# The second layer of eight experts as fifteen block products, with a fixed instruction order

## The chip, the core and the metric

The kernel runs on one core of a Trainium2 chip. A core has a matrix engine (TensorE, PE in the profile; its weight loads are PEld), three engines for elementwise work (VectorE = DVE, ScalarE = ACT, GpSimd = POOL), a queue engine (SyncE = SP) and 16 DMA engines that move data between the chip's main memory and the on-chip memory. Each engine takes its instructions in the order in which they stand in its own queue and waits on semaphores for the others. The metric is the device time of one execution in microseconds; three runs of the kernel before give a median of 415.86 us (415.71 to 416.34).

## The reference

An attention block with a decaying state gives a matrix `x` of 3072 tokens by 384 channels. Then each token goes to one of eight experts, 384 tokens to each, chosen by a greedy walk over all (token, expert) scores in falling order, and each expert is two matrix products with a relu between.

```python
def _moe_ref(x, w_gate, w1, w2):            # N, D, E, F = 3072, 384, 8, 1024
    cap = N // E
    logits = x @ w_gate
    order = np.argsort(-logits.flatten())
    for idx in order:                       # greedy walk
        tok, e = int(idx) // E, int(idx) % E
        if assigned[tok] >= 0 or counts[e] >= cap:
            continue
        assigned[tok] = e
        counts[e] += 1
    for e in range(E):
        mask = assigned == e
        h = np.maximum(x[mask] @ w1[e], 0.0)
        out[mask] = h @ w2[e]
```

## The kernel before

The first 165 us are the attention (class `Mild`) and, beside its end, 256 tokens of one expert chosen ahead of time (`Experts.early`); this change leaves both nearly alone. What follows is the part in question: seven experts with 384 tokens, then the remaining 128 tokens of the expert chosen early.

One full expert is, on TensorE:
- layer one, `hidden` (L1487): 8 blocks `j` of 128 hidden channels. Each is 3 matmuls with a 128x128 block of `w1` as weights and `xT`, 128 channels by 384 tokens, as the moving side, into `h_ps`; ScalarE applies the relu into `hid` (L1494).
- layer two, `result` (L1501): 3 blocks `c` of 128 tokens. Each is 8 matmuls with a 128x128 block of `hid` as weights and 128x384 of `w2` as the moving side, into `o_ps`. ScalarE copies the result to `o_sb`, and GpSimd scatters its rows to the output with an indirect DMA.
- before the last of the three, `turn` (L1477): nine transposes of the next expert's gathered tokens `xg` into `xT`.

Which expert comes next and which tokens it has is found by the class `Assignment` while the experts run. `likely_steps` (L977) is one search: three rounds of `count`, in each of which VectorE builds an indicator `ind`, TensorE counts it (`counts`, two matmul groups with VectorE's `own`, `cnt`, `wide` between them), and VectorE derives the next digit of a threshold; then two short matmuls into `st_ps` from which VectorE numbers the places. `book`, `choose` and `leave` are small VectorE steps on the result, and `leave` strikes the chosen tokens from the score table `LG`. `bound` (L1237) runs once: a matmul into `high_ps` and a reduction into `lowest`, which `book` reads. `tokens` (L1348) turns places into a list: VectorE builds `row` and `vals`, TensorE multiplies them (`some_ps`), VectorE reduces to `part`, TensorE multiplies once more (`list_ps`), and VectorE writes `tok`. `fetch` (L1473) then gathers the tokens by three indirect DMAs on GpSimd's queue, and has SP load the expert's two weight matrices of 1.5 MB each. The last search is `remainder` (L1315), which only takes what is left.

`run` (L1513) drives the experts and `later` (L1620) is the generator that yields the next one. In the attention part the order of the instructions is written out by hand (`tc.manual_schedule()`). From `x.run` on it is not: a scheduler places the search's instructions among the experts' matmuls. The weights are double buffered in two pools (`turns`), the searches' PSUM tiles share one buffer (tag `few`) and another for `counts`.

Of the kernel before, what the change touches and what calls it, by code (L numbers as in the profile page):

```python
# [688 lines left out]
class Assignment:  # L689
# [260 lines left out]
    def last_fill(self):  # L950
        out = self.remainder()
        return out["fmax"], self.tokens(out["place"])
# [290 lines left out]
    def surely(self, pool, fmax, acc, place):  # L1243
# [69 lines left out]
        self.places(pool, sel, acc, place)  # L1313

    def remainder(self):  # L1315
# [6 lines left out]
        fmax = self.outs.tile([128, 1], F32, name="fmax")  # L1322
        nc.vector.tensor_scalar(out=fmax, in0=self.last, scalar1=-1.0, scalar2=float(self.E),
                                op0=ALU.mult, op1=ALU.add)
        acc = self.outs.tile([128, self.NT], BF16, name="acc")
        place = self.outs.tile([128, self.NT], I32, name="place")
        self.places(pool, sel, acc, place)
        return dict(fmax=fmax, acc=acc, place=place)

    def places(self, pool, sel, acc, place):  # L1330

        nc, ps, NT = self.nc, self.ps, self.NT
        flat = sel.rearrange("p j i -> p (j i)")
        st_ps = ps.tile([128, 2, 2 * NT], F32, name="st_ps2", tag="few")
        nc.tensor.matmul(st_ps[:, 0, :], self.ones, flat, start=True, stop=True)
        nc.tensor.matmul(st_ps[:, 1, :], self.rest_of, flat, start=True, stop=True)
        upto = pool.tile([128, 2 * NT], F32, name="upto2")
# [10 lines left out]
    def tokens(self, place, NC=None):  # L1348

# [19 lines left out]
        self.between()  # L1369
# [36 lines left out]
def rwkv5_eagle_then_base_layer_balanced(  # L1406
# [31 lines left out]

    class Experts:
# [7 lines left out]
        def open_rest(self, ctx, **how):  # L1447
            pool = lambda name, bufs, **kw: ctx.enter_context(tc.tile_pool(name=name, bufs=bufs, **kw))
            self.h, self.o = pool("f_h", 2, **how), pool("f_o", 3, **how)
            self.ps_t, self.ps_h, self.ps_o = (pool(f"f_ps_{x}", 2, space=PSUM) for x in "tho")  # L1450

        def load_weights(self, n, fmax):
# [4 lines left out]
            w1, w2 = pool.tile([128, KD, F], F32, name="w1"), pool.tile([128, KF, DX], F32, name="w2")  # L1457
            e = nc.values_load(number[0:1, 0:1], engines=(mybir.EngineType.SP,), min_val=1, max_val=E,
                               skip_runtime_bounds_check_because="held between 1 and E")
            for t, src in ((w1, moe_w1), (w2, moe_w2)):  # L1460
                nc.sync.dma_start(t, src[ds(E - e, 1)].rearrange("o (c p) f -> p (o c) f", p=128))
            return w1, w2

# [9 lines left out]
        def fetch(self, n, fmax, tok):  # L1473
            xg = self.gather(n, tok)
            return n, xg, walk.in_order(tok), *self.load_weights(n, fmax)

        def turn(self, ahead):  # L1477
# [7 lines left out]
            return xT  # L1485

        def hidden(self, w1, xT, m):  # L1487
            hid = self.h.tile([128, KF, CAP], F32, name="hid")
            for j in range(KF):
                h_ps = self.ps_h.tile([128, CAP], F32, name="h_ps")  # L1490
                for f in range(KD):
                    nc.tensor.matmul(h_ps[:, 0:m], w1[:, f, ts(j, 128)], xT[:, f, 0:m],  # L1492
                                     start=(f == 0), stop=(f == KD - 1))
                nc.scalar.activation(hid[:, j, 0:m], h_ps[:, 0:m], AF.Relu)  # L1494
            return hid
# [5 lines left out]
        def result(self, c, hid, w2, tok, to):  # L1501
            o_ps = self.ps_o.tile([128, DX], F32, name="o_ps")
            for j in range(KF):
                nc.tensor.matmul(o_ps, hid[:, j, ts(c, 128)], w2[:, j, :], start=(j == 0), stop=(j == KF - 1))  # L1504
# [8 lines left out]
        def run(self, ahead, later, rows):  # L1513
            xT = self.turn(ahead)
            while ahead:
                _, _, tok, w1, w2 = ahead
                nb = tok.shape[1]
                ahead = next(later, None)
                hid = self.hidden(w1, xT, nb * 128)
                for c in range(nb):  # L1520
                    if c == nb - 1 and ahead:
                        xT = self.turn(ahead)
                    self.result(c, hid, w2, tok, next(rows))

        def early(self, ps, pool, w1, w2, xg, tok, rows, have):
# [18 lines left out]
            for c in range(NE):  # L1544
                o_ps = ps.tile([128, DX], F32, name="e_o_ps", tag=("y_ps", "g_ps")[c % 2])
                for j in range(KF):
                    nc.tensor.matmul(o_ps, hid[:, j, ts(c, 128)], w2[:, j, :], start=(j == 0), stop=(j == KF - 1))  # L1547
# [7 lines left out]
    with ExitStack() as whole:  # L1555
# [6 lines left out]
        with ExitStack() as part:  # L1562
# [20 lines left out]
            with tc.manual_schedule():  # L1583
# [22 lines left out]
                to = walk.in_order(tok)  # L1606
# [6 lines left out]
                for m in (2, 3, 2, 3):  # L1613
                    next(search)
                    go(m)
                go(99)
# [3 lines left out]
        def later():  # L1620
            for _ in search:
# [61 lines left out]
```

## Time and profile before

| what | us |
|---|---|
| median of three runs | 415.86 |
| the profiled run's own time | 415.83 |
| the span of the profiled execution | 414.1 |
| TensorE busy in the span | 394.4 |
| VectorE / ScalarE / GpSimd busy | 200.0 / 153.6 / 134.6 |
| one full expert, from first layer-one matmul to the next expert's | 33.4 |
| layer one's matmuls in all, 384 records | 122.2 |
| layer two's matmuls in all, 352 records | 117.6 |

The profile is one execution, taken by the hardware profiler. Lines of its group table read: source line, engine, operation, output tile and inputs, shapes, number of records, busy time, mean ns of one. A mean duration of one matmul is its latency; since matmuls are pipelined, the spacing of their starts is what a stream costs. Lines of the timeline read: start, duration, engine, line, operation, and in brackets how long the engine had been idle and what ended that. Lines of time windows list, for each engine, busy time and the number of records, then TensorE's granted clock, the share of time in which the DMA engines were busy, and GB/s. Lines of the chain of waits give the start and the length of a piece of the chain that ended last.

### The profile page before, as it was taken

The numbers are of one execution on the slowest core, as the hardware profiler recorded it, in microseconds if no ns is written. First come the engines' busy times: TensorE is split into PE (matmuls) and PEld (weight loads), VectorE is DVE, ScalarE is ACT, GpSimd is POOL, SyncE is SP. The second block draws the span as 40 slices with busy tenths as digits, with TensorE's granted clock in tenths as the row PEclk, the third lists the DMA queues.
The fourth block names the chain that finished last, engine by engine and source line by source line (L and its number), as shares of the span: only waits on it lengthen the run. The fifth ranks groups of instructions, "written<-read, shape, count | busy, mean of one in ns | idle before, by whom it ended". The sixth has DMA issues, their size and how long they took to land.

```text
span 414.1 us, 7993 instructions
## 1 busy us (share of the span) xinstructions
PE 394.4 (95%) x2981; PEld 268.3 (65%) x2981; DVE 200.0 (48%) x794; ACT 153.6 (37%) x401; POOL 134.6 (33%) x172
## 2 busy tenths in 40 slices
PE   5999999999999888999999999999999999999993
PEld 4778888888877655555556555555655655655581
DVE  5776776576885788780580381273074050010000
ACT  2597888788872312212121120221221221212120
POOL 5597878566732022004104103103002121110100
PEclk9799999999999999999999999999999999999998
DMA  9999998887591282047045137109108653350010
GB/s 123 163 154 195 197 169 153 157 169 156 123 321 41 78 298 101 2 142 258 21 180 201 38 91 291 39 10 352 38 21 311 240 173 109 138 190 5 19 39 25
DMA packets 95298, 57.25 MB, mean 138 GB/s; under 512 B 77201, under 2 KB 89490, under 8 KB 95250
## 3 DMA queue, kind: packets, MB, share of 16 engines
q1 hardware_dynamic: 91520, 47.19, 45.7%
q0 software_dynamic: 3072, 9.44, 6.4%
q8 instruction: 25, 0.41, 0.4%
q14 instruction: 23, 0.19, 0.2%
q10 hardware_dynamic: 658, 0.01, 0.1%
HBM read 47.20 MB, written 9.44 MB: 137 GB/s over the span
## 4 chain that ended last, share of the span: by engine, by line
PE 71%; DMA 12%; DVE 6%; issue 5%; ACT 2%; POOL 1%; POOLq 0%; ACTq 0%; DVEq 0%
PE h_ps L1492 21%; PE o_ps L1504 19%; DMA out_dram<-o_sb,to 11%; PE y_ps L532 7%; PE g_ps L494 5%; PE kT_ps L456 3%; PE kv_ps L511 3%; PE rT_ps L462 2%; PE x_ps L581 2%; PE e_o_ps L1547 2%; PE lg_ps L561 2%; PE xT_ps L1483 2%; ACT AT L484 1%; PE e_h_ps L1539 1%; POOL xg L1468 1%
## 5 line engine op out<-in xcount | busy, mean ns | idle before, releaser
L1492 PE MATMUL h_ps<-xT,w 128*128 128x384 f32 (+1 forms) x384 | 122.2, 469 | 0.6 <-ACT xT L1484 0.6
L1504 PE MATMUL o_ps<-w,hid 128*128 128x384 f32 x352 | 117.6, 487 | 0.0
L1504 PEld LDWEIGHTS o_ps<-w,hid 128*128 128x128 f32 x352 | 65.4, 190 | 42.4 <-issue 0.8
L1492 PEld LDWEIGHTS h_ps<-xT,w 128*128 128x128 f32 x384 | 65.6, 190 | 36.5 <-issue 3.6
L1494 ACT ACTIVATE hid<-h_ps 128x384 f32<-128x384 f32 (+1 forms) x64 | 29.7, 464 | 92.2 <-PE h_ps L1492 85.3
L484 ACT ACTIVATE AT<-ident,dd 128x128 f32<-128x128 f32 x192 | 58.7, 390 | 2.1 <-DVE dd L443 1.9
L1468 POOL DMA_INDIRECT xg<-x_rows,tok x22 | 21.3, 966 | 116.2 <-issue 58.9
L1498 POOL DMA_INDIRECT out_dram<-o_sb,to x21 | 20.8, 993 | 98.1 <-ACT o_sb L1510 66.4
L1510 ACT COPY o_sb<-o_ps 128x384 f32<-128x384 f32 x21 | 10.1, 479 | 95.5 <-PE o_ps L1504 86.8
L498 DVE COPY_PREDICATED AT<-mask,g_ps 128x512 f32<-128x512 uint8 x48 | 32.6, 734 | 12.5 <-PE g_ps L494 12.2
L889 DVE TENSOR_TENSOR own<-counts,same 128x64 f32<-128x64 f32 x21 | 4.7, 225 | 65.5 <-PE counts L901 65.5
L494 PE MATMUL g_ps<-rT,kT 48*128 48x128 f32 x384 | 28.2, 287 | 0.6 <-DVE AT L498 0.6
L431 POOL TENSOR_TENSOR kss<-krs,wk 128x384 f32<-128x384 f32 x24 | 24.3, 1015 | 10.7 <-DVE krs L340 9.0
L494 PEld LDWEIGHTS g_ps<-rT,kT 48*128 48x128 f32 x384 | 23.6, 189 | 3.8 <-PE rT_ps L462 0.8
L532 PE MATMUL y_ps<-AT,vts 128*64 128x128 f32 x384 | 25.7, 276 | 0.0
L438 POOL TENSOR_TENSOR rk<-rk,u_bc 128x384 f32<-128x384 f32 x24 | 24.2, 1008 | 3.7 <-ACT u_bc L407 1.9
L437 POOL TENSOR_TENSOR rk<-krs 128x384 f32<-128x384 f32 x24 | 24.5, 1019 | 0.0
L532 PEld LDWEIGHTS y_ps<-AT,vts 128*64 128x64 f32 x384 | 20.6, 137 | 1.0 <-issue 0.5
L550 ACT COPY x<-y_ps 128x512 f32<-128x512 f32 x24 | 14.0, 585 | 15.9 <-PE y_ps L532 15.9
L474 DVE TENSOR_TENSOR rT<-rT_ps,WR 112x512 f32<-112x512 f32 x23 | 15.8, 685 | 4.4 <-PE rT_ps L462 4.3
L462 PE MATMUL rT_ps<-ident,krs 128*112 128x128 f32 x96 | 15.3, 285 | 0.0
L581 PE MATMUL x_ps<-ident,x 112*128 112x112 f32 x96 | 13.3, 262 | 1.4 <-ACT xr L588 0.7
(270 smaller groups left out, 464.6 us busy)
## 6 DMA issues: line engine op xcount, KB each, us to landing
w<-in_moe_w_dram SPq DMA_DIRECT2D x18, 1536.0 KB, 8.3
krs<-in_k_dram SPq DMA_DIRECT2D x24, 192.0 KB, 4.1
krs<-in_r_dram SPq DMA_DIRECT2D x24, 192.0 KB, 4.7
vts<-in_v_dram SPq DMA_DIRECT2D x24, 192.0 KB, 4.5
x_rows<-xr SPq DMA_DIRECT2D x24, 192.0 KB, 2.9
xg<-x_rows,tok POOLq DMA_INDIRECT x22, 4.7
out_dram<-o_sb,to POOLq DMA_INDIRECT x21, 2.6
wp<-in_w_dram SPq DMA_DIRECT2D x2, 0.4 KB, 2.0
```

What stands on the lines that cost most here:

```text
L431: self.nc.gpsimd.tensor_mul(self.kss[:, n % self.NS].rearrange("p (g h) d -> p g h d", g=2)[:, :, :, 0:D], src, self.wk.rearrange("p (g h) ...
L437: nc.gpsimd.tensor_mul(rk, self.krs[:, n % self.NK, 1, 0:H, 0:D], self.krs[:, n % self.NK, 0, 0:H, 0:D])
L438: nc.gpsimd.tensor_mul(rk, rk, self.u_bc)
L462: nc.tensor.transpose(rT_ps[0:P, a, :], self.pair(kr[:, 1], a), self.ident)
L484: nc.scalar.mul(AT[:, z, a, :], self.ident, dd[:, h:h + 1])
L494: nc.tensor.matmul(g_ps[:, z, a, :], kT[rows, a, :], rT[rows, a, :], start=True, stop=True)
L498: nc.vector.copy_predicated(out=AT[:, z], mask=self.mask.unsqueeze(1).to_broadcast([128, HP, T]), data=g_ps[:, z])
L532: nc.tensor.matmul(yv[q * PD:(q + 1) * PD, o // 2, o % 2, :], lhsT, rhs, start=(o // 2, q) not in seen, stop=stop, skip_group_check=True)
L1468: nc.gpsimd.indirect_dma_start(out=xg[:, c, :], out_offset=None, in_=x_dram[0:within, :], in_offset=bass.IndirectOffsetOnAxis(ap=tok[:, c: ...
L1492: nc.tensor.matmul(h_ps[:, 0:m], w1[:, f, ts(j, 128)], xT[:, f, 0:m], start=(f == 0), stop=(f == KD - 1))
L1494: nc.scalar.activation(hid[:, j, 0:m], h_ps[:, 0:m], AF.Relu)
L1504: nc.tensor.matmul(o_ps, hid[:, j, ts(c, 128)], w2[:, j, :], start=(j == 0), stop=(j == KF - 1))
```

## The change

For the seven full experts the second layer is no longer 24 matmuls of 128x384. The 384x1024 matrix of hidden values is cut into 3 token blocks by 2 halves of the hidden channels (`h0` to `h5`), the 1024x384 weights into 2 halves by 3 blocks of output channels (`w0` to `w5`), and the 3x3 blocks of the result are made from fifteen products of sums of these blocks instead of eighteen products of the blocks. Each product is 4 matmuls of 128x128. The sums of hidden blocks (11 of 128x512) and of results (20 of 128x128) are made on VectorE. Ten sums of weights are made without an engine's addition: ScalarE copies one block, and a DMA on GpSimd's queue adds another block to the copy while it is moved. So that a weight block is contiguous, `w2` is laid out by blocks and loaded by six DMAs instead of one. Each group of four products shares one PSUM tile, which ScalarE copies to `res`.

```diff
+        W2_SUMS = (("W7", "w0", "w1"), ("W12", "w0", "w2"), ("W11", "w0", "w3"), ("W9", "W7", "w3"),
+                   ("W5", "W12", "w3"), ("W13", "W9", "w4"), ("W6", "W5", "w5"), ("W0", "W13", "w5"),
+                   ("W2", "W6", "w4"), ("W14", "W0", "w2"))
+        PRODUCTS = ((("p4", "h4", "w1"), ("p1", "H1", "w2"), ("p11", "H11", "W11"), ("p10", "h5", "w4")),
+                    (("p8", "H8", "w5"), ("p13", "h1", "W13"), ("p7", "H7", "W7"), ("p9", "H9", "W9")),
+                    (("p3", "H3", "w3"), ("p0", "H0", "W0"), ("p14", "h2", "W14"), ("p5", "H5", "W5")),
+                    (("p12", "H12", "W12"), ("p6", "H6", "W6"), ("p2", "H2", "W2")))
+        def w2_sums(self, w2, at):
+            for name, a, b in self.W2_SUMS:
+                t = self.sums.tile([128, KF // 2, 128], F32, name=name)
+                nc.scalar.copy(t, at[b])
+                nc.gpsimd.dma_start(out=t, in_=at[a], accum_op=ALU.add)
+                at[name] = t
+                yield
+        def hid_sums(self, at, which):
+            for name, a, op, b in which:
+                t = self.sums.tile([128, KF // 2, 128], F32, name=name)
+                nc.vector.tensor_tensor(out=t, in0=at[a], in1=at[b], op=op)
+        def products(self, left, right):
+            for group in self.PRODUCTS:
+                ps = self.ps_o.tile([128, 4, 128], F32, name="p_ps", tag="o_ps")
+                for q, (name, a, b) in enumerate(group):
+                    for j in range(KF // 2):
+                        nc.tensor.matmul(ps[:, q, :], left[a][:, j, :], right[b][:, j, :],
+                                         start=(j == 0), stop=(j == KF // 2 - 1))
+                    if q == len(group) - 1:
+                        nc.scalar.copy(res[:, n:n + q + 1, :], ps[:, 0:q + 1, :])
+                    yield res
...
-            for t, src in ((w1, moe_w1), (w2, moe_w2)):
-                nc.sync.dma_start(t, src[ds(E - e, 1)].rearrange("o (c p) f -> p (o c) f", p=128))
+            nc.sync.dma_start(w1, moe_w1[ds(E - e, 1)].rearrange("o (c p) f -> p (o c) f", p=128))
+            rows_of = moe_w2[ds(E - e, 1)].rearrange("o (j c p) (k f) -> p j k (o c) f", p=128, j=2, f=128)
+            for j in range(2):
+                for k in range(KD):
+                    nc.sync.dma_start(w2[:, j, k], rows_of[:, j, k])
```

The second part of the change puts the experts under `tc.manual_schedule()` too. `run` now counts layer one's 24 matmuls by `u` and the products by `q`, and at fixed values of both it asks `later` for the next step of the search, issues the block sums, and transposes the next expert's tokens. A step ends at a `yield`, which stands behind the TensorE instruction that the step leads to; so each search matmul has a fixed place. The first and the second full expert have plans of their own.

```diff
+        USUAL = (4, 7, 12, 19), (21, None), (1, 3, 11, 14), 8
...
+                for u in range(KF * KD):
...
+                    if f == KD - 1:
+                        nc.scalar.activation(hid[:, j, 0:m], h_ps[:, 0:m], AF.Relu)
+                        if j < KF // 2:
+                            next(sums, None)
+                            next(sums, None)
+                    if u in steps:
+                        next(later, None)
+                    if u == 5:
+                        next(out, None)
+                    if u == 8:
+                        to = walk.in_order(tok)
+                    if u == last[0]:
+                        ahead = found()
+                    if u == KF * KD - 2:
+                        for _ in sums:
+                            pass
+                        if nb == NC:
+                            self.hid_sums(left, self.FIRST_SUMS)
...
+                for q, res in enumerate(self.products(left, right)):
+                    if q in next_steps:
+                        next(later, None)
+                    if q == last[1]:
+                        ahead = found()
+                    if q == 1:
+                        self.hid_sums(left, self.SECOND_SUMS)
+                    if q == 3:
+                        self.hid_sums(left, self.THIRD_SUMS)
+                    if q == 11 or q == 14:
+                        next(out)
+                    if q == turned and ahead:
+                        xTs = self.turn(ahead)
+                    xT = next(xTs, xT)
...
+        first_plan = (2, 5, 8, 12, 14, 17, 19, 22), (None, 8), (6, 11, 13), 12
+        second_plan = (1, 3, 6, 8, 13, 20), (22, None), (1, 3, 11, 14), 9
+        with tc.manual_schedule():
+            x.run((1, xg, tok, *have["v"]), later(), (a for a in [*out_rows[2:NT - 1], None]),
+                  {"start": None, 1: first_plan, 2: second_plan})
```

`later` yields in more places, `tokens` and `remainder` are cut into steps, and the weights of the next expert are loaded as soon as its number is known, before its token list. The three scatters of an expert now come together, from one tile of 384 tokens, after the third group of result sums (`u == 5` of the next expert). The last 128 tokens keep the old second layer.

## The prediction

> **What bounds the kernel now.** I read first the page's busy table and slices, then the time windows over one expert, then the chain of waits in order of time, then the timeline of the last, small expert, which holds the one row that has the new products' shape.
>
> ```profile
> PE 394.4 (95%) x2981; PEld 268.3 (65%) x2981; DVE 200.0 (48%) x794; ACT 153.6 (37%) x401; POOL 134.6 (33%) x172
> PEclk9799999999999999999999999999999999999998
> ...
> 199.20:232.60 33.40, 33.40 (x128) 19.61 (x128) 14.21 (x74) 6.57 (x14) 5.93 (x6) 1.00 0.36 130
> ...
> 209.81 4.61 PE h_ps L1492 x14
> 214.42 0.15 PE some_ps L1365 x6
> 214.57 1.38 PE h_ps L1492 x4
> 215.96 10.42 PE o_ps L1504 x32
> 226.38 0.66 PE xT_ps L1483 x6
> ```
>
> The window 199.20 to 232.60 is one expert: TensorE (second figure) is busy for all 33.40 us at a granted clock of 1.00, VectorE 14.21, ScalarE 6.57, GpSimd 5.93, transfers 0.36 of the time. The chain there is TensorE alone, expert after expert. So the stage pays for the stream of matmul instructions, and anything that makes TensorE wait is paid in full. An f32 matmul of the source is two records here (24 of layer two make 48), a transpose one.
>
> **The products (gain).** Before: 24 matmuls of 384 columns, 48 records per expert. The chain gives 10.42 us for 32, so 0.3256 each and 15.63 us. After: 15 products of 4 matmuls of 128 columns, 120 records, each with its own weight load. That shape is in the trace: layer one of the last expert has 128 tokens.
>
> ```profile
> 396.64 5.52 PE L1492 MATMUL h_ps<-xT,w 128*128 128x128 f32 x48
> 400.85 0.28 ACT L1494 ACTIVATE hid<-h_ps 128x128 f32<-128x128 f32 x1 [0.39 <-PE h_ps L1492]
> 401.52 0.28 ACT L1494 ACTIVATE hid<-h_ps 128x128 f32<-128x128 f32 x1 [0.39 <-PE h_ps L1492]
> ```
>
> Relus follow each other by 0.67 us for 6 records: 0.1117 each, so 120 take 13.40 us. The gain is 2.23 us an expert, 15.6 us over the seven full experts. Bounds: 5.52/48 = 0.115 gives 13.8 and 12.8 us in all; a third of 0.3256 gives 13.0 and 18.2 us.
>
> The Trainium skill, "TensorE: Matmul & The Clock Gate", section "Back-to-back issue gap", speaks against the change: a stream of weight load and matmul is sustained at about 81 ns for 128 columns and 131 for 512, so small ones pay far more per column. Read linearly that is an estimated 114 ns at 384: 120 x 81 against 48 x 114 ns, 4.2 us lost an expert. The rows of this trace have the f32 shapes themselves, 0.1117 against 0.3256, almost in the ratio of the columns, and they decide.
>
> **The sums of hidden blocks and results.** 11 sums of 128x512 and 20 of 128x128 go to VectorE. No row has 128x512 from two SBUF tiles; TENSOR_TENSOR rows of 768 columns (944 ns) and 192 (344 ns) give 1.04 ns a column, 677 ns, and records overlap by some 0.07, so 0.61 each (0.55 to 0.68), and 0.21 to 0.28 for 128 columns. About 6.7 + 5 us join the 14.2: 26 of 31, so VectorE fits, but the order of its queue is now fixed, and so is the place of each search matmul on TensorE. ScalarE gets ten copies (0.585 each, the row of a 128x512 copy) and four PSUM copies for three: 6.6 becomes some 13 us. Two copies follow each of the first four relus, 0.49 + 1.17 us against a relu every 1.94: hidden; without that cover 0.3 us a relu.
>
> **Where the fixed order makes TensorE wait.** In the first full expert:
>
> ```profile
> 167.52 0.38 PE L1239 MATMUL high_ps<-ident,e_high 128*128 128x128 f32 x2
> 167.74 0.81 PE L1492 MATMUL h_ps<-xT,w 128*128 128x384 f32 x2
> 168.39 0.25 PE L901 MATMUL counts<-prop,ind 128*128 128x64 bf16 x3
> ```
>
> (a) Before, high_ps and the next search's first counts are 0.87 us apart, with layer one between: VectorE did the search's m, prop and ind first. After, both matmuls stand back to back behind layer one's sixth, and VectorE's queue puts the read of high_ps ahead of book, leave and the whole start of the search. From the spacings of those rows: high_ps to `lowest` 0.51, `lowest` twice 0.4, book 1.1, leave 1.3, cand, m, prop and low 0.9, ind to counts 0.8: 5.0 us, less 0.22 for high_ps itself, so 4.8 (3.9 to 5.2) in which layer one stands queued behind it. st_ps at the 23rd matmul adds 0.3.
> (b) The first list (some_ps) stands after the seventh product. VectorE has before it all 11 hidden sums (6.7) and the 3.1 us from `sole` to `vals`; TensorE gets there 7.1 us after st_ps: it waits 2.9. Then the token list, three gathers (spaced 1.27, landing 2.9 to 4.6 us after issue by the rows' least and usual), and the transposes placed after products 13 to 15: a further 1.3 to 2.9, the now uncovered copy of the last transposed block (0.8) included. Together 5.0 (4.2 to 5.8).
> (c) The second expert's result sums (1.75) stand between two search steps only 1.94 apart on TensorE: 1.3 (0 to 1.7).
> (d) In the five later experts the walk leaves 0.2 each, where the first two search steps meet VectorE's sums: 1.0 (0 to 4).
>
> **The sums of weights.** Ten copies, then ten accumulating 256 KB transfers on GpSimd's queue, five deep (W7, W9, W13, W0, W14), each issue waiting for the landing before it; three scatters and three gathers stand in the same queue. No row has an accumulation. Nearest:
>
> ```profile
> xg<-x_rows,tok POOLq DMA_INDIRECT x22, 4.7
> out_dram<-o_sb,to POOLq DMA_INDIRECT x21, 2.6
> ...
> 217.17 0.99 POOL L1468 DMA_INDIRECT xg<-x_rows,tok  x1 [16.21 <-issue]
> 218.46 0.96 POOL L1468 DMA_INDIRECT xg<-x_rows,tok  x1 [0.30 <-issue]
> ```
>
> An issue takes 0.97 and the next comes 1.27 later. A 192 KB scatter lands after 2.6; at the windows' 400 GB/s it moves in 0.5, 256 KB in 0.66, or twice that if the target is read too: 2.8 to 3.4, I take 3.0, nearest the scatter since most of the chain runs while no weights load; 2.6 and 4.6 are the ends. Walking the queue from an expert's first matmul: W7 3.3, W12 4.6, W11 5.9, W9 7.2, scatters to 11.0, W5 12.2, W13 13.5, W6 15.2, W0 16.5, gathers to 20.4, W2 21.7, W14 23.0, landed 26.0. Product 11 needs it at 15.5 + 0.5 (search) + 8.9 + 0.7 (transposes) + small waits = 25.9. So it costs nothing at 3.0, with no slack: 0.4 an expert at 3.2, 0.8 at 3.4, 2.8 at 4.2, 4.0 at 4.6, over six experts (the first has no scatters in the way). The gathers, queued ahead of W2, still land before their transposes.
>
> By the skill's "DMA: Bandwidth & Descriptors", section "Anatomy of one DMA — SWDGE (gpsimd) path", about 2.0 us plus bytes/436e3, each would take an estimated 2.6 us; no run yet shows an accumulation, and with that figure this term stays 0.
>
> Loading second-layer weights as six transfers costs SP six issues of 0.37 for one, on a queue with little else, and rows of 512 bytes; even at 163 GB/s, a rate of the slices where rows of 192 bytes move, 1.5 MB takes 9.4 us, and the load is issued some 17 us before use.
>
> **Sum**, against the span of 414.1: -15.6 + 4.8 + 0.3 + 5.0 + 1.3 + 1.0 + 0 = -3.2, so 410.9. The run of that profile took 415.83, 0.03 under the median of 415.86; 415.86 - 3.2 = **412.7**.
>
> **Rivals.** *The weight sums are late* (slower): accumulations land at about 4.2, as the gathers beside loading weights suggest; product 11 waits 2.8 us in six experts, 16.8, so 429.5. For it: the end of the chain runs beside the next weights' load. Against it: its first half runs with transfers idle, and the scatter row is 2.6. It decides from a landing of about 3.3 on, where 0.53 x 6 eats the 3.2. *The fixed order costs nothing*: VectorE's sums and searches fit and terms a to d vanish, 415.86 - 15.6 = 400.3. Against it: the built order shows high_ps and counts adjacent. *Small products pay for their weight loads*: 120 records at the 0.190 of an f32 LDWEIGHTS row, 22.8 for 15.63, seven times +7.2: 466. Against it: the small expert's 48 loads and matmuls both fit in 5.6 us.
>
> **How the numbers follow.** Forecast 0.50, late weight sums 0.37, no cost of order 0.10, weight loads 0.03. The forecast's own range: 406.1 (a to d at their lower ends, gain 18.2) to 417.3 (upper ends, gain 15.6). The range reaches part of the way into the late case: 403 to 424. A measurement of this kernel can tell about 0.2%, 0.83 us, from no change. Of the forecast some 0.38 lies below 415.0, 0.09 within, 0.03 above; the late case has 0.02 faster (barely late), 0.03 within, 0.32 above. With the others: faster 0.50, within 0.12, slower 0.38.
>
> **What would show it.** In the changed profile: 120 records of 128 columns per expert at 0.11 spacing; experts three to six about 31.2 us apart for 33.4; one idle stretch of 4 to 5 us of TensorE in front of counts soon after the first full expert starts, and 3 us before the first some_ps; product 11 (W14) as the only product that waits for a transfer. It is wrong if accumulations land later than 3.3 us, if one issue holds GpSimd well over 1 us, or if the products' spacing is above 0.12.

## The result, and the profile after

The changed kernel takes 479.97 us (median of four runs, 474.45 to 482.38), the kernel before, run beside it, 415.84; the ratio is 1.145, 95% interval 1.138 to 1.152. Ratios leave out the profiled run and any other more than 1.5% above the fastest: here two of the four (the other two average 476.2 us), and below two of the six with a ninth transfer. The forecast was 412.7 us in a range of 403 to 424; it was wrong by 67 us, to the slow side. The profiled execution spans 480.3 us.

From the page of the changed kernel, the busy table, the granted clock in 40 slices, the software queue's share and the landing times of the weight sums:

```profile
PE 406.6 (85%) x3485; PEld 320.3 (67%) x3485; DVE 291.2 (61%) x1011; ACT 195.7 (41%) x478; POOL 199.4 (42%) x242
...
PEclk8899999999999979879997997998899799799889
...
q0 software_dynamic: 13152, 27.79, 27.5%
...
W<-W POOLq DMA_DIRECT2D x49, 256.0 KB, 5.1
W<-w POOLq DMA_DIRECT2D x21, 256.0 KB, 3.4
```

TensorE was busy for 95% of the span before, and for 85% now: it waits, which behind the attention it hardly did before (1.3 us in all). What it waits for from 160 us on (engine, line, releaser, us in all, times, longest):

```profile
PE p_ps L1551 <- DMA W<-W: 22.7, 11, 5.3
PE xT_ps L1505 <- DMA xg<-x_rows,tok: 21.2, 6, 5.0
PE some_ps L1380 <- DVE vals L889: 5.8, 2, 4.8
PE counts L901 <- DVE ind L889: 5.7, 3, 4.2
```

The two lower rows are the forecast's terms (a), (c), (d) and the first half of (b). The two upper ones, 43.9 us, are products waiting for weight sums, and transposes waiting for gathered tokens; of these the forecast had only the wait for tokens in the first full expert (4.33 us here). Experts three to six are 40 to 42 us apart; before, it was 32.6 to 33.4, and the forecast expected 31.2.

One such expert, by its window (columns as before: TensorE's busy time second, then the granted clock, the DMA share, GB/s):

```profile
259.70:299.60 39.90, 33.56 (x200) 25.88 (x199) 27.11 (x104) 12.71 (x25) 15.48 (x16) 0.91 0.74 175
```

SP's and GpSimd's own timelines inside it show why:

```profile
271.55 0.37 SPq L1477 DMA_DIRECT2D w<-in_moe_w_dram  x1
272.50 9.89 SPq L1481 DMA_DIRECT2D w<-in_moe_w_dram  x6
```

```profile
271.75 1.90 POOL L1534 DMA_DIRECT2D W<-W  x2
280.92 0.85 POOL L1534 DMA_DIRECT2D W<-W  x1 [7.27 <-ACT res L1554]
282.55 0.85 POOL L1534 DMA_DIRECT2D W<-W  x1 [0.78 <-issue]
283.70 1.52 POOL L1491 DMA_INDIRECT xg<-x_rows,tok  x1 [0.30 <-DVE H L1541]
...
287.90 1.01 POOL L1534 DMA_DIRECT2D W<-W  x1
290.84 0.89 POOL L1534 DMA_DIRECT2D W<-W  x1 [1.93 <-DMA W<-W]
```

W5 and W13 go out at 271.75, 12.1 us after the expert's first matmul, which is where the forecast's walk had them (12.2). But the next expert's weights begin to load at 271.55, the same moment. W6 needs W5, and stands idle in GpSimd's queue for 7.27 us (the releaser named in the bracket had long been done). The chain of waits in order of time names such landings: each start and length is a piece of the chain that ended last.

```profile
272.37 9.40 DMA W<-W
...
282.55 7.74 DMA W<-W
...
290.84 3.45 DMA W<-W
...
294.33 1.36 PE p_ps L1551 x8
```

Two landings of 9.40 (W13) and 7.74 us (W0) beside the load, one of 3.45 us (W14) after it. The gathers, queued behind W0, go out 6 to 7 us later than the walk had them (24.0 to 27.2 us into the expert for 17.8 to 20.4), and TensorE stands:

```profile
290.92 0.90 PE L1505 MATMUL xT_ps<-ident,xg 128*128 128x128 f32 x3 [5.01 <-DMA xg<-x_rows,tok]
291.62 1.92 PE L1551 MATMUL p_ps<-W,H 128*128 128x128 f32 x8
```

and is then slow: the next transpose starts 1.71 us after that product's first record, where 0.89 is usual. The windows around it give the clock:

```profile
286.00:290.90 4.90, 0.00 (x0) 0.00 (x0) 2.03 (x8) 0.00 (x0) 2.67 (x4) 0.70 1.11 285
290.90:293.00 2.10, 2.08 (x10) 2.08 (x11) 0.00 (x0) 0.48 (x1) 0.83 (x1) 0.50 0.64 115
293.00:295.00 2.00, 1.84 (x10) 1.44 (x10) 0.00 (x0) 0.48 (x1) 0.00 (x0) 0.56 0.36 61
295.00:297.00 2.00, 2.00 (x22) 1.99 (x21) 0.00 (x0) 0.53 (x2) 0.00 (x0) 1.00 0.00 0
```

The granted clock (the figure behind the five engines) falls to half during the wait and stays there for some four microseconds behind it. The Trainium skill says in "TensorE: Matmul & The Clock Gate", section "What's actually happening", that an idle window of about 3.4 us brings the gate to half rate and that a busy one of the same length opens it. The rows show both rates and an end some four microseconds after the products resume; but a mean of 0.70 over the 4.90 us of waiting puts the fall some 2 us into the wait, sooner than after an idle window of 3.4. The forecast did not price it.

### The profile page after: what moved, and what is told of

The parts are those of the page before. It is cut to its first block, busy times and chain, and to the rows that moved or that the text cites. A ratio compares the mean times of both kernels' runs of the same rounds, so it can differ in the third digit from the quotient of the medians.

```text
span 480.3 us, 9678 instructions
## 1 busy us (share of the span) xinstructions
PE 406.6 (85%) x3485; PEld 320.3 (67%) x3485; DVE 291.2 (61%) x1011; ACT 195.7 (41%) x478; POOL 199.4 (42%) x242
## 3 DMA queue, kind: packets, MB, share of 16 engines
q0 software_dynamic: 13152, 27.79, 27.5%
## 4 chain that ended last, share of the span: by engine, by line
PE 43%; DMA 28%; issue 12%; DVE 10%; POOL 3%; ACT 3%; POOLq 0%; ACTq 0%; DVEq 0%
DMA W<-W 24%; PE h_ps L1625 11%; PE y_ps L532 6%; PE p_ps L1551 5%; PE g_ps L494 4%; PE e_o_ps L1692 2%; PE kv_ps L511 2%; PE kT_ps L456 2%; POOL out_dram L1583 2%; PE rT_ps L462 2%; PE x_ps L581 2%; PE lg_ps L561 1%; DMA xg<-x_rows,tok 1%; DMA W<-w 1%; DVE H L1541 1%
## 5 line engine op out<-in xcount | busy, mean ns | idle before, releaser
L1534 POOL DMA_DIRECT2D W<-W x49 | 43.9, 946 | 78.0 <-DMA W<-W 33.9
L1551 PE MATMUL p_ps<-W,H 128*128 128x128 f32 x448 | 67.0, 309 | 0.0
L1551 PEld LDWEIGHTS p_ps<-W,H 128*128 128x128 f32 x448 | 63.7, 225 | 0.2 <-issue 0.2
L1534 POOL DMA_DIRECT2D W<-w x21 | 18.4, 984 | 87.8 <-ACT W L1533 87.4
L1554 ACT COPY res<-p_ps 128x512 f32<-128x512 f32 (+1 forms) x28 | 15.6, 559 | 94.6 <-PE p_ps L1551 94.6
L498 DVE COPY_PREDICATED AT<-mask,g_ps 128x512 f32<-128x512 uint8 x48 | 32.7, 736 | 12.5 <-PE g_ps L494 12.2
L1551 PE MATMUL p_ps<-W,hid 128*128 128x128 f32 x112 | 20.5, 340 | 22.7 <-DMA W<-W 22.7
L1491 POOL DMA_INDIRECT xg<-x_rows,tok x22 | 23.4, 1063 | 39.0 <-issue 20.4
L1533 ACT COPY W<-w 128x512 f32<-128x512 f32 x70 | 39.5, 614 | 0.0
L1570 DVE TENSOR_TENSOR o_all<-res 128x128 f32<-128x128 f32 x63 | 17.1, 290 | 31.1 <-ACT res L1554 29.6
L1551 PEld LDWEIGHTS p_ps<-W,hid 128*128 128x128 f32 x112 | 17.5, 239 | 25.7 <-DMA W<-W 25.7
L1505 PE MATMUL xT_ps<-ident,xg 128*128 128x128 f32 x66 | 15.4, 361 | 22.1 <-DMA xg<-x_rows,tok 21.2
L1541 DVE TENSOR_TENSOR H<-hid 128x512 f32<-128x512 f32 x42 | 27.0, 685 | 11.0 <-ACT hid L1628 11.0
L1506 ACT COPY xT<-xT_ps 128x384 f32<-128x384 f32 x22 | 10.4, 479 | 57.0 <-PE xT_ps L1505 57.0
L494 PE MATMUL g_ps<-rT,kT 48*128 48x128 f32 x384 | 27.9, 285 | 0.6 <-DVE AT L498 0.6
L1583 POOL DMA_INDIRECT out_dram<-o_all,to x21 | 21.2, 1011 | 16.3 <-DVE o_all L1570 8.0
```

The lines of the kernel that those rows point to most:

```text
L494: nc.tensor.matmul(g_ps[:, z, a, :], kT[rows, a, :], rT[rows, a, :], start=True, stop=True)
L498: nc.vector.copy_predicated(out=AT[:, z], mask=self.mask.unsqueeze(1).to_broadcast([128, HP, T]), data=g_ps[:, z])
L1505: nc.tensor.transpose(xT_ps[:, f, :], xg[:, c, ts(f, 128)], ident)
L1533: nc.scalar.copy(t, at[b])
L1534: nc.gpsimd.dma_start(out=t, in_=at[a], accum_op=ALU.add)
L1541: nc.vector.tensor_tensor(out=t, in0=at[a], in1=at[b], op=op)
```

## The experiments

All ratios are against the kernel before, run beside each kernel (its medians lie between 415.8 and 416.2 us).

### The parts alone

**No weight sums.** The products read plain blocks where they would read sums.

```diff
-                t = self.sums.tile([128, KF // 2, 128], F32, name=name)
-                nc.scalar.copy(t, at[b])
-                nc.gpsimd.dma_start(out=t, in_=at[a], accum_op=ALU.add)
-                at[name] = t
+                at[name] = at[b]
```

> Leaves out the ten sums of weights: each product takes one plain weight block in place of its sum; everything else stays. Theory 1 (the sums arrive late, and with them the gathers queued behind them): products and transposes no longer wait for transfers, experts three to six are 31 to 32 us apart instead of 40 to 42, total 413 to 420. Theory 2 (the fixed order's waits for VectorE, not the sums, are the loss): total stays above 440.

Measured: 423.38 us, 1.017 (1.015 to 1.019). The sums of weights cost 56.6 us of the 64 (52.8 of 60 with the 476.2 us above), and without them the changed kernel is still 7 us over the kernel before. One expert in its middle:

```profile
279.70:310.90 31.20, 31.20 (x201) 24.29 (x199) 27.37 (x107) 7.61 (x15) 6.17 (x7) 1.00 0.45 140
```

31.20 us at full clock with TensorE never idle: the gain of 2.2 us an expert is there, as forecast. What eats it is the first full expert, 51.2 us long (34.3 before). TensorE's three longest kinds of wait in this run, 15.0 us together, and a window over that expert:

```profile
PE some_ps L1380 <- DVE vals L889: 5.7, 2, 4.8
PE counts L901 <- DVE ind L889: 5.7, 3, 4.2
PE xT_ps L1505 <- DMA xg<-x_rows,tok: 3.6, 1, 3.6
...
164.00:215.00 51.00, 37.89 (x206) 29.25 (x206) 35.02 (x144) 7.37 (x15) 3.91 (x4) 0.87 0.26 78
```

**The fixed order alone**, with the second layer as it was (24 matmuls of 384 columns) and no block sums at all.

```diff
+        def old(self, hid, w2, tok, rows):
...
-                sums = self.w2_sums(w2, right) if nb == NC else iter(())
+                sums = iter(())
...
-                for q, res in enumerate(self.products(left, right)):
+                for q, _ in enumerate(self.old(hid, w2, to, rows)):
...
```

> The fixed order alone: layer two is again 24 matmuls of 384 columns with the search steps at like places, no block sums. By the forecast's terms only the wait for high_ps's reader (4.2 to 4.8 and 0.3) and little else stays, with 1 to 2 us at a lower clock behind it: total 420 to 425. If the fixed order costs nothing 414 to 417; if it is the main loss, above 440.

Measured: 424.13 us, 1.019 (1.016 to 1.021), with TensorE's 4.24 us before the counts again. By itself the order costs 8 us.

**The products alone**, the experts left to the scheduler.

```diff
-        with tc.manual_schedule():
+        if True:
             x.run((1, xg, tok, *have["v"]), later(), (a for a in [*out_rows[2:NT - 1], None]),
```

> The fifteen products with their sums, but the experts left to the scheduler's order instead of the fixed one (part one of the change alone). Theory (the sums cost by their chain and their place, which the scheduler does not know to be slow): 440-490 us. Rival (the fixed order is what makes the sums late): 425 us or less.

Measured: 427.03 us, 1.025 (1.020 to 1.029). The theory fell, and the rival, about the fixed order, comes far nearer (2 us above its range). Products alone cost 11 us, the order alone 8, both 60 to 64: over 40 us arise only where they meet. ScalarE's timeline in this run shows what the scheduler did otherwise:

```profile
261.38 0.62 ACT L1533 COPY W<-w 128x512 f32<-128x512 f32 x1 [6.52 <-DMA w<-in_moe_w_dram]
261.90 0.58 ACT L1554 COPY res<-p_ps 128x512 f32<-128x512 f32 x1
...
276.87 0.48 ACT L1554 COPY res<-p_ps 128x384 f32<-128x384 f32 x1 [0.28 <-PE p_ps L1551]
```

The copies of the next expert's blocks start at 261.38, as soon as they land, between the copies of this expert's products, whose last is at 276.87. The chain has a head start of half an expert. The fixed order pins it behind the expert's own first relus.

### What it is about the weight sums

**Sums made, but unread**, and **sums made of plain blocks, so unchained, and unread**:

```diff
+            at.update({name: at["w" + str(i % 6)] for i, (name, _, _) in enumerate(self.W2_SUMS)})
+            at = {k: v for k, v in at.items() if k[0] == "w"}
             for name, a, b in self.W2_SUMS:
...
-                nc.scalar.copy(t, at[b])
-                nc.gpsimd.dma_start(out=t, in_=at[a], accum_op=ALU.add)
-                at[name] = t
+                nc.scalar.copy(t, at.get(b, at['w4']))
+                nc.gpsimd.dma_start(out=t, in_=at.get(a, at["w3"]), accum_op=ALU.add)
```

(the first two lines are both runs', the rest is the second's)

> The changed kernel with all ten copies and ten accumulating transfers issued as before, but the products read plain blocks of the weights instead of the sums (so the second layer's result is left out of being right: it is the product of other blocks). TensorE then waits for no sum; what is left of their cost is the traffic and the place in GpSimd's queue. Theory (the gathers stand in GpSimd's queue behind sums that wait for sums, and land late): the waits on W vanish, waits of 3-6 us on the gathered rows stay in five experts, 436-455 us. Rival (it is the waits on the sums alone): 422-428 us, as with the sums left out (423.4 us).

> The changed kernel with ten copies and ten accumulating transfers of the same size in the same places, but each adds two plain blocks, so that no transfer waits for another, and the products read plain blocks (the second layer's result is of other blocks). Beside the run in which the sums were chained and unread (457.4 us) it tells the chain from the traffic. Theory (the gathers are late because GpSimd's queue stands still at each sum that waits for the landing of another): without the chain the gathers land in time, 422-432 us, waits on the gathered rows under 2 us. Rival (20 MB more through the DMA engines slow the gathers and the load whatever their order): 440-457 us, waits on the gathered rows of 4 us and more.

Measured: 457.43 us (1.100, 1.097 to 1.103) with the chain, 428.11 us (1.030, 1.026 to 1.033) without it. So in steps: ten copies and transfers an expert cost 4.7 us (428.11 - 423.38), the chain 29.3 us though TensorE reads none of it, and reading the sums another 22.5 (18.7 with 476.2). The wait that the chain makes, and the landings of the transfers (least, middle and longest), in the first of these runs and then in the second:

```profile
PE xT_ps L1505 <- DMA xg<-x_rows,tok: 28.6, 5, 6.8
DMA to landing us min/median/max: 3.3/4.4/11.0
...
PE xT_ps L1505 <- DMA xg<-x_rows,tok: 7.6, 5, 3.5
DMA to landing us min/median/max: 3.3/6.3/12.7
```

A sum that waits for another's landing holds GpSimd's queue, and the gathers that stand behind it go out late. Slow landing alone does not do it: unchained, the transfers land later still (6.3 us in the middle against 4.4), and it hardly matters. What the traffic does show is how full the DMA engines get (the unchained run again, one window):

```profile
259.00:290.00 31.00, 30.06 (x193) 23.39 (x193) 26.88 (x103) 11.54 (x24) 14.24 (x15) 1.00 0.91 216
```

A share of 0.91 over 31 us, against 0.45 without the sums: 14 us more of all 16 engines for nine or ten transfers, an estimated 1.5 us each. The page's software queue gives the same for the changed kernel: 27.5% of 480.3 us, against 6.5% of 420.4 without the sums, is 105 us more for 70 transfers.

**Sums on GpSimd** in place of copy and transfer.

```diff
-                nc.scalar.copy(t, at[b])
-                nc.gpsimd.dma_start(out=t, in_=at[a], accum_op=ALU.add)
+                nc.gpsimd.tensor_tensor(out=t, in0=at[a], in1=at[b], op=ADD)
```

> The ten sums of weights are additions on GpSimd instead of a copy and an accumulating transfer. Theory 1: 1.3 to 1.5 us each by the 1.015 us of a 128x384 product there, 14 us of an expert's 31, no landing in the chain; experts 31 to 33 apart, total 415 to 425. Rival (VectorE and GpSimd hold each other up with two on-chip inputs each): additions of 2 us or more, VectorE's sums over 0.8, experts 35 or more apart, total above 440.

Measured: 487.32 us, 1.170 (1.168 to 1.173). From the groups of this run (busy, then mean ns of one):

```profile
L1540 DVE TENSOR_TENSOR H<-hid 128x512 f32<-128x512 f32 x42 | 37.8, 942 | 4.6 <-ACT hid L1627 4.6
...
L889 DVE TENSOR_TENSOR wide<-digit_of,cnt 128x128 f16<-128x128 f32 x21 | 25.0, 1191 | 0.7
```

and from the timelines of VectorE and GpSimd, a subtraction of one column while GpSimd adds:

```profile
282.90 5.50 DVE L889 TENSOR_TENSOR past_low<-low,cell 128x1 f32<-128x1 f32 x1
...
283.45 4.92 POOL L1533 TENSOR_TENSOR W<-W,w 128x512 f32<-128x512 f32 x4
```

GpSimd's own addition took 1269 to 1335 ns in the mean, less than the rival's 2 us. With transfers, the same sums of hidden blocks took 685 ns and `wide` 292. The searches lose more than the transfers cost. The Trainium skill says in "SBUF — State Buffer", section "Who interferes with whom", that a VectorE instruction with two inputs in the on-chip memory contends with a GpSimd instruction that reads it; these rows agree.

### Other places for the weight sums

**The next load later** (at the fourth product), and **the sums earlier as well** (three behind each relu):

```diff
+                    if q >= 3 and ahead and len(ahead) == 4:
+                        ahead = *ahead[:3], *self.load_weights(ahead[0], ahead[3])
...
                             next(sums, None)
                             next(sums, None)
+                            next(sums, None)
```

> The next expert's weights are asked for at the fourth product instead of layer one's twentieth matmul, some 5 us later, so that most of the sums run before the load. Theory 1a (contention: an accumulation lands in 3.3 us alone and in 7 to 10 beside the load): sums land in 3.3 to 4, the waits before the sixth and eleventh product shrink to under 1 us together, experts 33 to 35 us apart, total 425 to 445. Theory 1b (the chain of five is too slow by itself): waits stay, 38 or more apart, total above 460.

> The changed kernel with the same ten weight sums, moved out of the way of the next weights: three sums behind each relu instead of two (so that all ten stand in GpSimd's queue by the fourth relu), and the weights of experts 3 and later asked for at the fourth product instead of at the twentieth matmul of the first layer. Theory (the sums are cheap as long as they run alone: 3.3 us a landing, a chain of five, 16.5 us, which ends before the products that read it; what costs is that the late ones run beside the next expert's weights at 7 to 10 us and hold the gathers behind them): the experts in the middle come back from 40 to 31-33 us, the kernel at 424-436 us. Rival (ten accumulating transfers of 256 KB are too many for the time of one expert wherever they stand): still 455 us or more, with waits on W of the old size.

Measured: 479.36 us (1.154, 1.149 to 1.160) and 489.18 us (1.178, 1.174 to 1.181). Both theories fell. In the first, the queue runs up to the gathers nearly as the forecast's walk had it (third expert: W6 16.1 us after the first matmul for 15.2, the first gather 18.7 for 17.8). The last two sums, W2 and W14, now meet the load instead:

```profile
276.88 0.37 SPq L1477 DMA_DIRECT2D w<-in_moe_w_dram  x1
...
272.16 0.85 POOL L1534 DMA_DIRECT2D W<-W  x1 [2.11 <-ACT W L1533]
...
278.87 1.94 POOL L1534 DMA_DIRECT2D W<-W  x2
```

They land after 8.6 and 9.7 us, the product that reads W14 waits 5.4, and all waits on W grow from 22.7 to 27.9 us. In the second the waits on W shrink from 22.7 to 10.4 us, as meant, and the waits for gathered rows grow from 21.2 to 44.4: with all ten sums ahead of the gathers, those go out behind the whole chain and meet the load.

```profile
281.73 0.86 POOL L1534 DMA_DIRECT2D W<-W  x1 [0.89 <-DMA W<-W]
282.90 1.18 POOL L1491 DMA_INDIRECT xg<-x_rows,tok  x1 [0.31 <-issue]
```

Waits were moved more than removed.

**Another order in the first full expert**, without the sums; then with them, together with the edits just named.

```diff
-        first_plan = (2, 5, 8, 12, 14, 17, 19, 22), (None, 8), (6, 11, 13), 12
+        first_plan = (2, 8, 10, 15, 17, 20, 22), (None, 6), (0, 5, 11, 13), 12
...
-                    if q == 3:
+                    if q == (6 if n == 1 else 3):
                         self.hid_sums(left, self.THIRD_SUMS)
...
+                if n == 2:
+                    next(steps)
+                    yield
+                    next(steps)
+                    walk.bound(ident)
+                    walk.book(was)
+                    yield
```

> The kernel without the ten weight sums (as in the run that left them out, 423.4 us) with another order in the first full expert alone: the searched-out tokens leave the list and the next search starts before the bound and the bookkeeping (which go behind the search's second step), the search's steps are asked for later in the first layer (after matmuls 3, 9, 11, 16, 18, 21, 23 and the first product), and the second expert's list stands on VectorE ahead of the last seven sums of hidden blocks instead of behind them. Theory (the fixed order of the first expert costs 13-16 us there: 4.2 us before counts, 4.8 us before some_ps, 3.6 us before the gathered rows, and TensorE's lower clock after each): the first expert takes 37-40 us instead of 51, the kernel 408-413 us. Rival (VectorE simply has too much to do in the first expert, so that waits only move): the first expert 46-51 us, 418-424 us.

> Both together: the weight sums kept, three behind each relu, the next weights asked for at the fourth product, and the other order in the first full expert. Theory: what the two runs save adds up, 411-424 us, and if the sums are really hidden it ends within 3 us of the run without sums and with the other order. Rival (the sums cost by themselves): no better than 440 us.

Measured: 411.56 us (0.989, 0.987 to 0.991), as the theory had it, and 476.13 us (1.145, 1.142 to 1.148), the rival. The first is a bound: with the weight sums left out, the change is worth 1.1% once its first expert's order is mended (40.8 us instead of 51.2). The second shows again that moving the load is no cure for the chain.

**The chain begun in the expert before**, then on top of it **w2 loaded ahead of w1** (with five sums ahead instead of four, in another order), and the changed load alone **under the scheduler**.

```diff
+                    if ahead and ahead[2].shape[1] == NC and q in ((14,) if n == 1 else (10, 11, 13, 14)):
+                        if coming is None:
+                            at = {}
+                            coming = at, self.w2_sums(ahead[4], at)
+                        next(coming[1])
```

> All ten weight sums kept and used, but begun one expert earlier: from the eleventh product of an expert on, the first four sums of the next one (W7, W11, W12, W9) are copied and sent, so that the other six stand in GpSimd's queue by the twelfth matmul of the next expert's first layer, before its gathers; the order of the first full expert is the one that gave 411.6 us without sums. Theory (a sum costs only where it runs beside the next weights' load and where a gather stands behind it): the chain of some 17-22 us lies between one load's end and the next one's start, waits on W and on the gathered rows shrink to 0-3 us an expert, 413-430 us. Rival (ten accumulating transfers don't fit beside an expert of 31 us at all): 440 us or more.

> As the run whose sums begin one expert earlier (437.35 us), with two moves more: the six transfers of w2 are asked for before the one of w1, so that the sums' blocks land first, and five sums (W7, W11, W9, W13, W12, the long chain first) go out between the eighth and the fourteenth product of the expert before. Theory (what was left there came from the next load and the last sums running into each other: w2 landed late, so the chain began late, so it ran into the next load again): the chain ends before the next load, waits on W vanish, 412-422 us. Rival (the DMA engines are simply full, 29 of 31 us an expert by their shares, so that no order hides the sums): 428-438 us.

> The fifteen products in the scheduler's order (427.03 us) with one edit: the six transfers of w2 before the one of w1. Theory (there ScalarE's copies waited for w2's landing, 6.5-8 us idle at the head of the chain, so the chain starts as early as w2 lands): 418-425 us. Rival (the order of the load is of no matter, the DMA engines are full): 426-429 us.

Measured: 437.35 us (1.049, 1.046 to 1.052), 439.86 us (1.056, 1.054 to 1.059) and 426.51 us (1.024, 1.020 to 1.027). The head start is worth 39 us over the run that shares its first expert (476.13; that one also loads late and sends three sums behind each relu). In the first of the three the third and fourth expert are 32.3 and 32.6 us apart, the three behind them 34.5 to 37.7, again with waits for gathered rows; the second expert, whose weights come too late for it, loses 9.7 us against the run without sums. Loading w2 first took the waits on W away and lengthened those for gathered rows (19.8 us): no gain, nor under the scheduler, where 0.5 us is inside the runs' scatter.

### Looking for a version that wins

On top of the run that loads w2 first (439.86 us), **eight transfers, two sums on VectorE** (W14 and W2, the chains' ends), then **the transposes later**, then **H9 ahead of the list** in the first full expert, then **nine transfers and one sum**:

```diff
+                if name in ("W14", "W2"):
+                    nc.vector.tensor_tensor(out=t, in0=at[a], in1=at[b], op=ADD)
...
-        USUAL = (4, 7, 12, 19), (21, None), (1, 3, 11, 14), 8
+        USUAL = (4, 7, 12, 19), (21, None), (1, 3, 11, 14), 11
...
+                    if n == 1 and q == 5:
+                        self.hid_sums(left, self.THIRD_SUMS[:1])
...
-                if name in ("W14", "W2"):
+                if name == "W14":
```

> The same with the two sums at the chains' ends (W14 and W2) made by VectorE (two of 0.69 us an expert, between its own sums) instead of by copy and accumulating transfer: eight transfers an expert, four deep. Theory (chain and traffic are what is left): 2 to 8 us faster than the ten transfers of the run beside it. Rival (VectorE has only some 2 us of idle time in an expert of 31 us, by the trace of the run without sums, and becomes the limit): the same or up to 5 us slower.

> The run with eight accumulating transfers and two sums on VectorE (425.77 us), with the transposes of the next expert's tokens behind the twelfth to fourteenth product instead of the ninth (the second expert: tenth) and the two after it. Theory (what is left there is mostly TensorE waiting 1 to 2 us at those transposes for gathered rows, 7.6 us in all, and a lower clock behind one of them): 412-418 us, at most 2 us of waits on gathered rows, so the changed kernel can be brought to about the kernel before. Rival (the rows come ever later as TensorE gets ahead, the DMA engines set the pace): 422-426 us, the waits the same in size.

> The same one product later still (behind the thirteenth, fourteenth and fifteenth product, so that the copy of the last transposed block stands before the next expert's first matmul). Theory: within 2 us of the run beside it, with 0.5-0.6 us for that copy in each of five experts. Rival: as beside it, 422-426 us.

> The best run so far (418.52 us: eight accumulating transfers begun one expert earlier, two sums on VectorE, transposes behind the twelfth product), with one of the sums of hidden blocks (H9) moved ahead of the list's last steps in the first full expert. Theory (its 2.23 us wait of the eighth product for H9, and TensorE's lower clock of 0.72 in the 6 us after it, are all that is left of the first expert's excess): 3 to 4.5 us less, 414-415.6 us, at or a little under the kernel before. Rival (the wait moves to the list and the gathers behind it): 417.5-419.5 us.

> The same with one sum on VectorE (W14) and nine accumulating transfers. Theory (in the middle experts, 32.0 us apart for 31.2 without sums, VectorE sets the pace: 0.66 us of waits before the counts): half of that 0.8 comes back, up to 2 us faster than the run beside it. Rival (a ninth transfer an expert makes the gathers late again): 2 to 8 us slower.

Measured: 425.77 us (1.025, 1.021 to 1.029); 418.52 us (1.005, 1.003 to 1.007) with the transposes behind the twelfth product, 421.54 us (1.013, 1.011 to 1.014) one later (the theory's range ended at 418); 418.61 us (1.006, 1.004 to 1.008) with H9 moved; 436.48 us (1.047, 1.044 to 1.049) with a ninth transfer. Two sums fewer in the queue return 14 us, more than expected, and the ninth transfer costs some 17. At 418.5 the middle experts look like this:

```profile
240.00:272.00 32.00, 31.34 (x200) 24.25 (x199) 28.26 (x108) 11.62 (x24) 12.81 (x14) 1.00 0.81 202
```

32.0 us against 31.2 without sums, the remaining 0.66 us a wait for VectorE before the counts. Moving H9 removed one wait of 2.23 us and made two others of 1.28 and 1.50. No version with all its sums beats the kernel before; the best is 0.5% behind it.

## Why the prediction was wrong

**Weight sums: 0 forecast, 56.6 us measured** (52.8 with 476.2). This is the step that failed: "I take 3.0, nearest the scatter since most of the chain runs while no weights load". Of the 19 landings that the changed kernel's trace has, the least is 3.3 us, at which the forecast itself asked for 0.53 an expert, the middle 4.3 and the longest 10.8; with all 70 on record, in the run with unread sums, they are 3.3, 4.4 and 11.0. The load does not meet the end of the chain but its middle: the walk put W5 at 12.2 us into the expert, it went out at 12.1, and the load began at 11.9. From there W6 slipped from the walk's 15.2 to 21.3, and W14's landing from 26.0 to 34.6. With the load moved to the fourth product, W6 was back at 16.1, and W2 and W14 were late in its place.

**"The gathers, queued ahead of W2, still land before their transposes"** fell with it. The walk had the gathers behind W0 in the sums' queue, but with 3.0 for every landing in front of them; the chain in front of the gathers cost 29.3 us with nobody reading it.

**The size of a transfer.** The forecast moved 256 KB in 0.66 us, twice that at most if the target is read. The DMA share gives an estimated 1.5 us of all 16 engines. Ten of these beside the load fill the engines to 0.91, and both get slower: the six transfers of w2 took SP 9.89 us to issue, against 6.4 to 6.6 (the last load 7.9) without sums and with the mended first expert. The forecast asked of the load only whether it was hidden; it was, but it was also what the chain ran into. The Trainium skill's figure ("DMA: Bandwidth & Descriptors", section "Anatomy of one DMA — SWDGE (gpsimd) path"), an estimated 2.6 us, is 0.7 us under even the least landing here; the measurement decides.

**The lower clock: not priced.** In the profiles the changed kernel waits 40.4 us more than the one without sums (55.4 against 15.0 in the four rows of waits), and its 1422 matmul records behind 164 us are busy for 254.84 us against 233.58. So about a third of the 59.9 us between the two profiles is not waiting but slow matmuls after it.

**Products: right.** -15.6 forecast; eight records of 128 columns follow each other by 0.893 us, which is 0.1117 each, and the middle experts without sums are 31.2 us apart, as it said. A record cost 3% more than a third of one of 384 columns (0.1117 against 0.1085), so the extra weight loads cost next to nothing.

**The fixed order: right in place, short in size.** Forecast 12.4 us (a to d, and 0.3). The run without sums has 423.38 for 416.24 - 15.6, so 22.7. (a) 4.24 us for 4.8. (b) 4.79 before `some_ps` and 3.63 before the gathered rows, 8.4 for 5.0. (c) 0.95 for 1.3. For (d), 1.0 spread over the five later experts, 0.49 more in the second expert and 0.93 in the sixth. The 0.3 at st_ps did not show. What is missing, 7.7 us, is mostly the clock behind the waits of the first expert: its window had a mean of 0.87.

**The rival of late weight sums** had the mechanism and the side, and a price of 16.8 us, about a third of the measured one, since it let one product wait and nothing else. Weight loads that are paid (466 us) came nearest in time and had nothing to do with it.

**Not settled.** Whether the ninth transfer's 17 us come from the engines' load or from one more link ahead of the gathers was not tried apart; nor was a weight load in rows longer than 512 bytes.

## What to carry to other kernels

Transfers that wait for each other hold their queue, and everything behind them in it, whoever reads them: before pricing a chain, list what stands behind each link in that queue, and what else runs at the same time as each link. A fixed order can cost far more than its parts where it takes from a chain the head start that a scheduler had found. And a wait of a few microseconds in a TensorE-bound stage is to be priced at more than its length, since the matmuls behind it can run at a lower clock (0.50 for some four microseconds behind a wait of 5.01 us here).

## What the runs showed of the hardware

An accumulating transfer of 256 KB within the on-chip memory landed 3.3 to 5 us after its issue with no weight load beside it and mostly 6 to 11 us beside one (the run with unread, chained sums), and takes an estimated 1.5 us of all 16 DMA engines; its issue holds GpSimd for 0.86 us in the middle. The half clock needs no single long wait. In the run without sums and with the mended first expert, waits of 0.99 and 2.23 us lie within four microseconds of each other, and the three products behind the second run at 0.228 us a record (granted clock 0.51 from 193.0 to 198.4):

```profile
189.43 0.31 PE L1380 MATMUL some_ps<-vals,row 128*128 128x48 f16 x6 [0.99 <-DVE vals L889]
189.58 1.14 PE L1548 MATMUL p_ps<-w,H 128*128 128x128 f32 x8
...
192.96 5.48 PE L1548 MATMUL p_ps<-w,H 128*128 128x128 f32 x24 [2.23 <-DVE H L1538]
```

In the first run with eight transfers, waits of 0.9 to 1.7 us before transposes left the clock at 1.00, and one of 1.95 us brought it to 0.72 in the six microseconds that follow.
